# A fused layer-norm, spectral filter and bilinear block: 512-row gate products, GpSimd sums and one weight queue

## The chip, the cores and the metric

The kernel runs on one core of a Trainium2 chip. Time is device time in microseconds (us). A profile adds one traced execution with its own span, 1.7 to 2.2 us shorter than the device time of the same run. Most executions of one kernel agree within 0.3%. A run counts as slow when it lies more than 1.5% above the fastest of the same kernel; every comparison below uses fast runs alone, and every traced execution was a fast one.

In the profile PE is TensorE (matrix products), PEld its weight loads, DVE is VectorE, ACT is ScalarE, POOL is GpSimd, SP is the engine that issues most transfers. L964 is line 964 of that kernel's file, so one and the same statement has different numbers in different kernels.

## The reference

```python
def _A_ref(x, w_r, w_i):                 # x: 1 x 2048 x 640, filter: 2048 x 321
    X = rfft2(x.astype(f32)) * (w_r + 1j * w_i)
    return irfft2(X, s=(S, D)).astype(bf16)

def _B_ref(x, w_gate, w_up, w_down):     # 640 x 1536, 640 x 1536, 1536 x 640
    h = (x @ w_gate) * (x @ w_up)
    return h @ w_down

xn = layernorm(x)                        # over the 640 columns
out = x + _A_ref(xn, w_r, w_i) + _B_ref(xn, w_gate, w_up, w_down)
```

There are 2048 rows, worked on as 16 blocks of 128. "Gate products" below means the products with both `w_gate` and `w_up`; "bilinear product" means the elementwise `g * u` on VectorE.

## The kernel before

The kernel doesn't leave order to chance: it registers some hundreds of tasks (with engine, estimated duration, priority, what they read and write, and which PSUM banks they take), and its own planner, at build time, simulates the engines and fixes **one instruction order per engine**. On the chip each engine runs its list in that order and waits on semaphores. PSUM banks (8 of them, used singly or as 4 pairs) are handed out in the plan too, and a class of tasks may have a cap on how many it holds at once:

```python
sch = _Sched()
sch.caps = {"glu": opts.get("cap_glu", 2), "acc": opts.get("cap_acc", 4), "fill": 1}
...                                                # in plan(), for each task that could go next:
cap = self.caps.get(t.cls)
if cap is not None and held_by_cls.get(t.cls, 0) >= cap:
    continue
```

The phases on TensorE: warm-up products with zeros; transposes of the normalised blocks 0 to 3; the row transform (R); a spectral stage of 16 blocks, each a first transform (D), a second one (C, 321 columns), a multiplication by the filter on VectorE, sums, and an inverse product (IA); the second inverse stage (I) with a lot of VectorE work; and the down products, which also add the last spectral product. **Gate products are the filler**: they have the lowest priority and take what the other stages leave free, until they run out. Then the down products begin.

The gate products, as they were, for two blocks (256 rows), gate and up side by side in one bank:

```python
_CHUNKS = ((0, 1), (1, 1), (2, 2), (4, 2), (6, 2), (8, 2), (10, 2), (12, 2), (14, 2))   # (first block, blocks)
...
for w in range(2):                                 # gate, up
    for j in range(5):                             # 640 = 5 x 128
        ins = c.e.matmul(ps[:, bk, w * n:(w + 1) * n], v_gw[:, w, j, ft, :],
                         v_xt[:, j, rows], start=(j == 0), stop=(j == 4))
```

The sums of one spectral block, all on VectorE, behind that block's five multiplications:

```python
def em_cb(c, r2=r2):
    p00, p01, p10, p11 = (v_p[:, r2, 0, 0], ...)
    c.e.tensor_tensor(v_y[:, r2, 512:768], p01[:, 0:256], p10[:, 0:256], _OP.add)              # large
    c.e.scalar_tensor_tensor(v_y[:, r2, 896:961], p01[:, 256:321], -1.0, p10[:, 256:321], ...) # small
    c.e.tensor_tensor(v_y[:, r2, 768:833], p00[:, 256:321], p11[:, 256:321], _OP.subtract)     # small
    return c.e.tensor_tensor(v_y[:, r2, 256:512], p00[:, 0:256], p11[:, 0:256], _OP.subtract)  # large
```

The weight loads, gate weights on SP's queue, the first three of the up weights on ScalarE's:

```python
dma("ld_gw%d_%d" % (f0, w_), ..., q="act" if w_ and i < 3 else "sp")
```

Of the kernel before, what the change touches and what calls it, by code (L numbers as in the profile page):

```python
# [15 lines left out]
_DMA_LAT = 1300.0  # L16
_DMA_ISSUE = 520.0
# [53 lines left out]
class _Sched(object):  # L71
# [81 lines left out]
    def plan(self, nbanks=8, filler_deadline=0.0):  # L153
# [8 lines left out]
        eng_free = dict((e, 0.0) for e in _ENGS)  # L162
# [334 lines left out]
_OP = AluOpType  # L497
# [8 lines left out]
_CHUNKS = ((0, 1), (1, 1), (2, 2), (4, 2), (6, 2), (8, 2), (10, 2), (12, 2), (14, 2))  # L506
_LP = 321
_SN = math.sin(2.0 * math.pi / 5.0)
# [20 lines left out]
def _d_dve_tt16(n):  # L529
    return n * 0.52 + 75.0  # L530
# [16 lines left out]
def _build(nc, A_x, A_w_r, A_w_i, B_w_gate, B_w_up, B_w_down, out, opts=None):  # L547
# [3 lines left out]
    with es:  # L551
# [8 lines left out]
        sch.caps = {"glu": opts.get("cap_glu", 2), "acc": opts.get("cap_acc", 4), "fill": 1}  # L560
        lay = {}
# [43 lines left out]
        b_p = alloc("P", 2 * 4 * 2 * _LP)  # L605
        b_y = alloc("Y", 2 * 1024)
# [49 lines left out]
        v_p = V("P").bitcast(_F32).rearrange("p (r w c l) -> p r w c l", r=2, w=2, c=2)  # L656
        v_y = V("Y").rearrange("p (r n) -> p r n", r=2)
# [57 lines left out]
        dma("ld_sm1", v_sm[:, 1:3, :], d_sm[:, 1:3, :], 128 * 512, [(b_sm, ("t", 1, 3))], prio=0.25)  # L715
# [38 lines left out]
        for gi, (b0, nb) in enumerate(_LN_GROUPS):  # L754
            pbase = 1.0 + 0.05 * gi if gi < 4 else opts.get("ln_prio", 5.99) + 0.05 * (gi - opts.get("ln_lead", 3))
            for b in range(b0, b0 + nb):
                if b >= opts.get("act_stats", 8):
                    def em_sm(c, b=b):
                        return c.e.activation(v_jk, v_x[:, b, :], _ACTF.Copy, scale=1.0 / _D,
                                              accum_out=v_m32[:, b:b + 1])  # L760
                    T("sm%d" % b, "act", _d_act(640) + 93, em_sm, reads=[(b_x, ("s", b, b + 1))],
                      writes=[(b_m32, ("b", b, b + 1)), (b_jk, None)], prio=pbase)

                    def em_sq(c, b=b):
                        return c.e.activation(v_jk, v_x[:, b, :], _ACTF.Square, scale=-1.0, bias=v_m32[:, b:b + 1],
                                              accum_out=v_ss[:, b:b + 1])
                    T("sq%d" % b, "act", _d_act(640) + 186, em_sq,
                      reads=[(b_x, ("s", b, b + 1)), (b_m32, ("b", b, b + 1))],
                      writes=[(b_ss, ("b", b, b + 1)), (b_jk, None)], prio=pbase)
                else:  # L770
                    bns = []
                    for i in range(2):
                        def em_bn(c, b=b, i=i):
                            return c.e.bn_stats(v_st[:, b, 6 * i:6 * i + 6], v_x[:, b, 320 * i:320 * i + 320])  # L774
                        bns.append(T("bn%d_%d" % (b, i), "dve", 420.0, em_bn, reads=[(b_x, ("s", b, b + 1))],
                                     writes=[(b_st, ("b", 2 * b + i, 2 * b + i + 1))], prio=pbase))
                    if b == 1:
                        bns[0].deps.add(muls[0])
                        bns[1].deps.add(e0_first)

                    def em_ag(c, b=b):
                        return c.e.bn_aggr(v_mv[:, b, :], v_st[:, b, :])
                    T("ag%d" % b, "dve", 176.0, em_ag, reads=[(b_st, ("b", 2 * b, 2 * b + 2))],
                      writes=[(b_mv, ("b", b, b + 1))], prio=pbase)
            if b0 >= opts.get("act_stats", 8):
                def em_mb(c, sl_=slice(b0, b0 + nb)):
                    c.e.tensor_copy(v_mv[:, sl_, 0], v_m32[:, sl_])
                    return c.e.tensor_scalar(v_mv[:, sl_, 1], v_ss[:, sl_], 1.0 / _D, None, _OP.mult)
                T("mb%d" % b0, "dve", 211.0, em_mb, reads=[(b_m32, ("b", b0, b0 + nb)), (b_ss, ("b", b0, b0 + nb))],
                  writes=[(b_mv, ("b", b0, b0 + nb))], prio=pbase)  # L790
# [74 lines left out]
        for g in range(8):  # L865
            b = 2 * g
            gr = g % 2
            pf = opts.get("f_prio", 6.0) + 0.05 * g
# [67 lines left out]
        for i, (f0, nf) in enumerate(_GW_LOADS):  # L936
            for w_ in range(2):
                dma("ld_gw%d_%d" % (f0, w_), v_gw[:, w_, :, f0:f0 + nf, :].rearrange("p j r f -> p j (r f)"),
                    gvs[w_][:, :, f0 * 128:(f0 + nf) * 128], 5 * 128 * nf * 256,
                    [(b_gw, ("s", w_ * _NGW + f0, w_ * _NGW + f0 + nf))], prio=(0.004, 0.012, 0.022, 0.032, 0.05)[i] + 0.001 * w_,  # L940
                    q="act" if w_ and i < 3 else "sp")
        w_at = [6.0 + 2.2 * min(ft // 2, 4) for ft in range(12)]
        c_at = [6.3 + 2.2 * (b0 + nb - 1) for b0, nb in _CHUNKS]
        units = sorted((max(c_at[ci], w_at[ft + 1]), ci, ft) for ci in range(len(_CHUNKS)) for ft in range(0, 12, 2))
        for ui, (at_, ci, ft0) in enumerate(units):
# [5 lines left out]
            pe_ = 5.0 + 0.001 * ui  # L951
            for u in range(2):
                ft = ft0 + u

# [19 lines left out]
            def em_h(c, ft0=ft0, rr=rr, n=n, rows=rows):  # L974
                return c.e.tensor_tensor(v_ht[:, ft0:ft0 + 2, rows], v_gbf[:, rr, :, 0:n], v_gbf[:, rr, :, n:2 * n],  # L975
                                         _OP.mult)
            T("H_%d" % ui, "dve", _d_dve_tt16(2 * n), em_h,
              reads=[(b_gbf, ("r", 2 * rr, 2 * rr + 2))],
              writes=[(b_ht, ("col", b0, b0 + nb))], prio=pe_)
# [6 lines left out]
        for t in range(16):  # L986
            pq = 10.0 + 0.05 * t
            ar = t % 3
            r2 = t % 2
# [41 lines left out]
            def em_wm(c, tc=tc, r2=r2, wr=wr):  # L1031
                bk = bank_of(tc)
                ins = None
                for h in range(2):
# [3 lines left out]
                    for w in range(2):  # L1038
                        c.e.tensor_tensor(  # L1039
                            v_p[:, r2, w, :, 128 * h:128 * h + 128].rearrange("p c (m k) -> p c m k", k=4),  # L1040
                            xh.rearrange("p c (m k) -> p c m k", k=4), wv[:, w].unsqueeze(1).to_broadcast([128, 2, 32, 4]), _OP.mult)
                ins = c.e.tensor_tensor(  # L1042
                    v_p[:, r2, :, :, 256:321], ps[:, bk:bk + 2, 256:321].unsqueeze(1).to_broadcast([128, 2, 2, 65]),
# [4 lines left out]
                   writes=[(b_p, ("r", r2, r2 + 1))], prio=pq - 0.001, frees=tc)  # L1048
            hold(tc, wm)

            def em_cb(c, r2=r2):
                p00, p01, p10, p11 = (v_p[:, r2, 0, 0], v_p[:, r2, 0, 1], v_p[:, r2, 1, 0], v_p[:, r2, 1, 1])

                c.e.tensor_tensor(v_y[:, r2, 512:768], p01[:, 0:256], p10[:, 0:256], _OP.add)  # L1054
                c.e.scalar_tensor_tensor(v_y[:, r2, 896:961], p01[:, 256:321], -1.0, p10[:, 256:321], _OP.mult,
                                         _OP.subtract)
                c.e.tensor_tensor(v_y[:, r2, 768:833], p00[:, 256:321], p11[:, 256:321], _OP.subtract)
                return c.e.tensor_tensor(v_y[:, r2, 256:512], p00[:, 0:256], p11[:, 0:256], _OP.subtract)  # L1058
            T("CB_%d" % t, "dve", 2 * _d_dve(256) + 2 * _d_dve(65), em_cb,
              reads=[(b_p, ("r", r2, r2 + 1))], writes=[(b_y, ("r", 2 * r2, 2 * r2 + 1))], prio=pq - 0.001)  # L1060

            def em_ng(c, r2=r2):
                c.e.activation(v_y[:, r2, 0:256], v_y[:, r2, 512:768], _ACTF.Copy, scale=-1.0)  # L1063
                c.e.activation(v_y[:, r2, 833:896], v_y[:, r2, 897:960], _ACTF.Copy, scale=-1.0)
                return c.e.activation(v_y[:, r2, 961:1024], v_y[:, r2, 769:832], _ACTF.Copy)
            T("NG_%d" % t, "act", _d_act(256) + 2 * _d_act(63), em_ng,
              reads=[(b_y, ("r", 2 * r2, 2 * r2 + 1))], writes=[(b_y, ("r", 2 * r2 + 1, 2 * r2 + 2))],
              prio=pq - 0.001)

            def em_ia(c, t=t, r2=r2):  # L1070
                bk = bank_of(c.t)
                ins = None
                for k in range(5):
                    if k < 4:
                        l1, l2 = v_y[:, r2, 256 + k:768:4], v_y[:, r2, k:512:4]
                    else:
                        l1, l2 = v_y[:, r2, 768:896], v_y[:, r2, 896:1024]
# [4 lines left out]
            ia = T("IA_%d" % t, "pe", 10 * _d_mm(128), em_ia, reads=[(b_y, ("r", 2 * r2, 2 * r2 + 2)), (b_wd, ("e", 256 * t, 256 * t + 256))],  # L1082
# [14 lines left out]
        for a in range(16):  # L1097
            pa = 19.0 + 0.05 * a
# [71 lines left out]
        for a in range(16):  # L1170
            pc = 41.0 + 0.05 * a
# [3 lines left out]
            for hf in range(2):  # L1175
# [14 lines left out]
                def em_iv(c, ag2=ag2, a=a, sl3=sl3):  # L1190
# [3 lines left out]
                       reads=[(b_v, ("a", a, a + 1)), (b_sm, ("t", 1, 3))], prio=pc + 0.01 + 0.001 * hf - 22.0, after=[ag2])  # L1194

                def em_f1(c, ag2=ag2, a=a, xs=xs, sl3=sl3):
# [3 lines left out]
                       reads=[(b_xr, ("r", xs, xs + 1))], writes=[(b_out, ("r", ro, ro + 1))], prio=pc - 0.001,  # L1200
# [6 lines left out]
        sch.slack["dve"] = opts.get("slack_dve", 300.0)  # L1207
        sch.affinity = opts.get("affinity", 1500.0)
        sch.dma_bw = float(opts.get("dma_bw", 330.0))
        sch.plan(8, filler_deadline=opts.get("fill_deadline", 7000.0))  # L1210
# [77 lines left out]
```

## Time and profile before

| | kernel before |
|---|---|
| device time, median (range) | 210.78 us (210.69 to 210.83, 4 runs beside the changed kernel) |
| span of the traced execution | 209.1 us, clock 1.00 |
| TensorE, VectorE, ScalarE, GpSimd busy | 96%, 88%, 59%, 0% |
| first gate product | 7.38 us |
| spectral stage on TensorE: first D, last IA | 87.1, 140.8 us |
| last gate product | 145.2 us |

The prediction below shows the lines that carry most of this. One more is needed later, for the stretch from 90 to 125 us of the kernel before. It gives the stretch and its length, then busy us and instructions of TensorE, its weight loads, VectorE, ScalarE and GpSimd, then the granted clock, the DMA share and GB/s.

```profile
90.00:125.00 35.00, 34.42 (x383) 30.21 (x380) 33.89 (x112) 30.65 (x82) 0.00 (x0) 1.00 0.27 61
```

In the spectral stage TensorE (34.42 of 35) and VectorE (33.89) are both full. Such a line can't say which of the two is the bound; only what happens when one is relieved can.

### The profile page before, as it was taken

The page shows a single profiled execution, that of the slowest core. Times are in us where ns is not written, and L with a number is a line of the kernel's source. Part 1 is how long each engine was busy: PE and PEld are TensorE (multiplying, and loading weights), DVE is VectorE, ACT ScalarE, POOL GpSimd, SP SyncE. Part 2 cuts the span into 40 slices and gives each one's busy share as a digit, 9 for nine tenths or more (in the row PEclk, how much of TensorE's full clock was granted, in tenths as well). Part 3 has the DMA queues.
Part 4 walks back from the last instruction along what each step waited for, and adds up shares of the span by engine and source line. Part 5 has one row for each costly group of instructions (what it writes and reads, how often), then busy time and mean ns, then how long its engine had stood idle before and what let it go on. Part 6 is the DMA issues. An engine that isn't in the chain of part 4 may idle for free.

```text
span 209.1 us, 5208 instructions
## 1 busy us (share of the span) xinstructions
PE 201.7 (96%) x2044; PEld 170.5 (82%) x2044; DVE 184.3 (88%) x536; ACT 122.3 (59%) x281; POOL 0.2 (0%) x4
## 2 busy tenths in 40 slices
PE   7789999999999999989999999999999999999994
PEld 8689889988898998979888889898777776777773
DVE  4599999999999999389999999965999999999941
ACT  2276799899985666878998998888422022000000
POOL 0000000000000000000000000000000000000000
PEclk9999999999999999999999999999999999999999
DMA  6999983032011666102224223025022233223311
GB/s 178 301 340 391 383 113 68 5 63 58 9 31 35 141 198 178 33 17 57 52 57 122 53 61 103 0 66 157 3 75 71 78 110 110 56 88 110 91 55 47
DMA packets 30600, 21.74 MB, mean 104 GB/s; under 512 B 10480, under 2 KB 29552, under 8 KB 30448
## 3 DMA queue, kind: packets, MB, share of 16 engines
q1 hardware_dynamic: 28464, 20.40, 35.9%
q10 hardware_dynamic: 2112, 1.02, 1.9%
q8 instruction: 16, 0.26, 0.5%
q14 instruction: 8, 0.07, 0.1%
HBM read 16.82 MB, written 2.62 MB: 93 GB/s over the span
## 4 chain that ended last, share of the span: by engine, by line
PE 77%; DVE 9%; SPq 6%; DMA 5%; issue 2%; ACT 1%; DVEq 0%
PE ps L960 44%; PE ps L1183 17%; SPq L705 6%; DMA arena<-c_sm 5%; PE ps L921 2%; PE ps L1080 2%; PE ps L1079 2%; PE ps L1003 2%; PE ps L1191 1%; PE ps L1108 1%; PE ps L1024 1%; PE ps L1027 1%; PE ps L1026 1%; PE ps L1025 1%; DVE arena L1198 1%
## 5 line engine op out<-in xcount | busy, mean ns | idle before, releaser
L711 ACT ACTIVATE arena<-ps 128x512 bf16<-128x512 f32 (+5 forms) x190 | 100.6, 570 | 48.7 <-PE ps L960 21.8
L960 PE MATMUL ps<-arena 128*128 128x256 bf16 (+1 forms) x1080 | 112.0, 261 | 2.8 <-DMA arena<-in_B_w_gate_dram 1.0
L960 PEld LDWEIGHTS ps<-arena 128*128 128x128 bf16 x1080 | 93.7, 98 | 13.7 <-DMA arena<-in_B_w_gate_dram 1.9
L1183 PE MATMUL ps<-arena 128*128 128x320 bf16 x384 | 56.4, 299 | 0.0
L1183 PEld LDWEIGHTS ps<-arena 128*128 128x128 bf16 x384 | 37.3, 98 | 14.3 <-DVE arena L1198 0.2
L975 DVE TENSOR_TENSOR arena<-arena 128x512 bf16<-128x512 bf16 (+1 forms) x54 | 20.9, 389 | 9.5 <-ACT arena L711 9.3
L1039 DVE TENSOR_TENSOR arena<-ps,arena 128x256 f32<-128x256 f32 x64 | 22.6, 415 | 0.0
L1198 DVE TENSOR_TENSOR arena<-ps,arena 128x320 bf16<-128x320 f32 x32 | 15.4, 482 | 5.1 <-PE ps L1191 5.1
L1080 PE MATMUL ps<-arena 128*128 128x128 bf16 x80 | 10.7, 219 | 0.0
L1079 PE MATMUL ps<-arena 128*128 128x128 bf16 x80 | 10.6, 219 | 0.0
L774 DVE BATCH_NORM_STATS2 arena<-arena 128x6 f32<-128x320 bf16 x16 | 7.2, 478 | 3.4 <-DMA arena<-in_A_x_dram 3.2
L1079 PEld LDWEIGHTS ps<-arena 128*128 128x128 bf16 x80 | 8.8, 112 | 0.3
L1191 PE MATMUL ps<-arena 128*128 128x320 bf16 x32 | 8.9, 299 | 0.0
L874 DVE TENSOR_TENSOR arena<-arena 128x384 f32<-128x384 bf16 x16 | 8.8, 552 | 0.0
L1080 PEld LDWEIGHTS ps<-arena 128*128 128x128 bf16 x80 | 8.7, 112 | 0.1
L1042 DVE TENSOR_TENSOR arena<-ps,arena 128x260 f32<-128x260 f32 x16 | 7.0, 439 | 0.0
L1054 DVE TENSOR_TENSOR arena<-arena 128x256 bf16<-128x256 f32 x16 | 6.7, 420 | 0.2
L1063 ACT ACTIVATE arena<-arena 128x256 bf16<-128x256 bf16 x16 | 6.6, 411 | 0.4 <-DVE arena L1058 0.3
L875 DVE TENSOR_TENSOR arena<-arena 128x256 f32<-128x256 bf16 x16 | 6.7, 418 | 0.0
L1058 DVE TENSOR_TENSOR arena<-arena 128x256 bf16<-128x256 f32 x16 | 6.7, 417 | 0.0
L1163 DVE TENSOR_TENSOR arena<-arena 128x640 bf16<-128x640 f32 x8 | 6.5, 816 | 0.1
L1003 PE MATMUL ps<-arena 128*128 128x128 bf16 (+1 forms) x80 | 6.6, 219 | 0.0
(69 smaller groups left out, 208.1 us busy)
## 6 DMA issues: line engine op xcount, KB each, us to landing
arena<-in_A_x_dram SPq DMA_DIRECT2D x20, 160.0 KB, 2.4
out_dram<-arena SPq DMA_DIRECT2D x32, 80.0 KB, 1.6
arena<-c_tf SPq DMA_DIRECT2D x4, 384.0 KB, 10.9
arena<-in_A_w_r_dram SPq DMA_DIRECT2D x32, 40.1 KB, 2.3
arena<-in_A_w_i_dram SPq DMA_DIRECT2D x32, 40.1 KB, 2.2
arena<-in_B_w_gate_dram SPq DMA_DIRECT2D x4, 320.0 KB, 7.6
arena<-in_A_x_dram SPq DMA_DIRECT2D x1, 1280.0 KB, 12.2
arena<-c_ti SPq DMA_DIRECT2D x2, 512.0 KB, 4.7
```

The lines of the kernel that those rows point to most:

```text
L705: return c.e.dma_start(dst, src)
L711: return c.e.activation(dst, src, _ACTF.Copy)
L874: c.e.tensor_tensor(uo[:, o, :, 0:3, :], v_xb[:, b:b + 2, 0:6:2, :], v_xb[:, b:b + 2, 5:10:2, :], op)
L960: ins = c.e.matmul(ps[:, bk, w * n:(w + 1) * n], v_gw[:, w, j, ft, :], v_xt[:, j, rows], start=(j == 0), stop=(j == 4))
L975: return c.e.tensor_tensor(v_ht[:, ft0:ft0 + 2, rows], v_gbf[:, rr, :, 0:n], v_gbf[:, rr, :, n:2 * n], _OP.mult)
L1003: ins = c.e.matmul(psflat[:, bk * 512 + k * 128: bk * 512 + k * 128 + n], v_uq[:, k, t, :], v_fd[:, k * 128: k * 128 + n], start=True, sto ...
L1039: c.e.tensor_tensor(v_p[:, r2, w, :, 128 * h:128 * h + 128].rearrange("p c (m k) -> p c m k", k=4), xh.rearrange("p c (m k) -> p c m k", k ...
L1079: c.e.matmul(dst, l1, v_ti[:, t, 0, :], start=True, stop=False)
L1080: ins = c.e.matmul(dst, l2, v_ti[:, t, 1, :], start=False, stop=True)
L1183: ins = c.e.matmul(ps[:, bk, 0:320], v_ht[:, ft, a * 128:(a + 1) * 128], v_wd[:, ft, sl3], start=(ft == 7), stop=False)
L1191: return c.e.matmul(ps[:, bank_of(ag2), 0:320], v_sm[:, 2, :], v_v[:, a, sl3], start=False, stop=True)
L1198: return c.e.tensor_tensor(v_out[:, a % 2, sl3], ps[:, bk, 0:320], v_xr[:, xs, sl3], _OP.add)
```

## The change

The intent: fewer instructions on TensorE for the same gate work; VectorE relieved by an engine that stands idle; and gate weights in the order in which they are needed. In the plan this comes with third buffers and retuned constants. The core of the diff:

```diff
-_CHUNKS = ((0, 1), (1, 1), (2, 2), (4, 2), (6, 2), (8, 2), (10, 2), (12, 2), (14, 2))
+_CHUNKS = ((0,1),(1,1),(2,2),(4,4),(8,4),(12,4))
...
+                if nb == 4:                       # a bank holds gate or up for 512 rows
+                        for j in range(5):
+                            ins = c.e.matmul(ps[:, bk, :], v_gw[:, w, j, ft, :], v_xt[:, j, rows], ...)
...
+            def em_cd(c, ar=ar):                  # the two small sums, VectorE
+                c.e.scalar_tensor_tensor(v_y[ar][:, 896:961], ...)
+                return c.e.tensor_tensor(v_y[ar][:, 768:833], ...)
+            cd = T("CD_%d" % t, "dve", ...)
+            def em_cb(c, ar=ar):                  # the two large sums
+                c.e.tensor_tensor(v_y[ar][:, 512:768], p01[:, 0:256], p10[:, 0:256], _OP.add)
+                return c.e.tensor_tensor(v_y[ar][:, 256:512], p00[:, 0:256], p11[:, 0:256], _OP.subtract)
+            ce = opts.get("cb_eng", "pool")
+            T("CB_%d" % t, ce, ..., after=[cd])
...
-                    q="act" if w_ and i < 3 else "sp")
+                    q="act" if w_ and i < 1 else "sp")
...
+        sch.caps["a"] = opts.get("cap_a", 2)      # transforms may hold 2 of the 4 PSUM pairs
-        b_p = alloc("P", 2 * 4 * 2 * _LP)         # products of a block: a third buffer
+        b_p = alloc("P", 3 * 4 * 2 * _LP)
+        b_y3 = alloc("Y3", _YS, at=lay["STAT"][0])   # spectrum of a block: a third buffer
-        dma("ld_sm1", ..., prio=0.25)             # table of the first transform product: earlier
+        dma("ld_sm1", ..., prio=0.055)
...                                                # and of the planner's constants:
-_DMA_LAT = 1300.0
+_DMA_LAT = 1000.0
+_START = 680.0
-        sch.slack["dve"] = opts.get("slack_dve", 300.0)
-        sch.affinity = opts.get("affinity", 1500.0)
+        sch.slack["dve"] = opts.get("slack_dve", 600.0)
+        sch.slack["pe"] = opts.get("slack_pe", 1500.0)
+        sch.affinity = opts.get("affinity", 300.0)
...
```

Cut: some more constants of this kind (priorities of the normalisation and of the row transform, the end of the fillers, the assumed DMA rate and issue time), and the statistics of blocks 6 and 7, which go from VectorE to ScalarE.

> **What bounds the kernel now.** I read the page first, then the products by shape, then the chain of work that ended last, then TensorE's timeline at the start and in the middle, then busy time by stretches.
>
> ```profile
> span 209.1 us, 5208 instructions
> PE 201.7 (96%) x2044; PEld 170.5 (82%) x2044; DVE 184.3 (88%) x536; ACT 122.3 (59%) x281; POOL 0.2 (0%) x4
> ```
>
> TensorE (PE) is busy 96% of the span, VectorE (DVE) 88%, GpSimd (POOL) nothing. The run takes 210.76 us, 1.66 more than the span. "Busy" can hide slack, since pipelined products overlap, so I take the pace of products from unbroken runs in the chain of waits:
>
> ```profile
> 37.33 0.56 PE ps L921 x10
> 70.85 6.55 PE ps L960 x60
> 176.35 1.63 PE ps L1183 x12
> ```
>
> Columns: start, length, what. Ten 128-column products take 0.56 us (56 ns each), sixty 256-column gate products 6.55 (109.2 ns), twelve 320-column down products 1.63 (135.8 ns). All three fit columns / 2.4 + 2.5 ns. So TensorE's own need is a sum. Gate: 840 x 109.2 + 240 x 56 ns = 105.1 us. Down and last spectral product: 416 x 135.8 = 56.5. Other 128-column products (transposes, four transform stages): 420 x 56 = 23.5. The 64 of 321 columns, 136.5 ns apart in the timeline: 8.7. Together 193.8 us, at a granted clock of 1.00.
>
> The rest of the span is loss, and TensorE's timeline at the start shows half of it (the bracket is idle time and what ended it):
>
> ```profile
> 6.59 0.22 PE L729 MATMUL ps<-arena 128*128 128x128 bf16 x1
> 7.38 1.29 PE L960 MATMUL ps<-arena 128*128 128x128 bf16 x20 [0.57 <-DVE arena L795]
> 9.66 1.29 PE L960 MATMUL ps<-arena 128*128 128x128 bf16 x20 [0.98 <-DMA arena<-in_B_w_gate_dram]
> 10.78 0.44 PE L835 MATMUL ps<-arena 128*128 128x128 bf16 x5
> 11.84 2.48 PE L960 MATMUL ps<-arena 128*128 128x128 bf16 x40 [0.61 <-DVE arena L782]
> ...
> 24.24 0.73 PE L921 MATMUL ps<-arena 128*128 128x128 bf16 x10 [0.25 <-DMA arena<-c_sm]
> ```
>
> Before 7.38 us there are only warm-up products, fillers (L729) and one transpose. Comparing start-to-start with the pace above, the issue stream then loses 1.16 us before 9.66, 0.78 before 11.84, about 0.4 in small pieces, and 0.41 before 24.24: 2.75 us. After 25 us I find only 0.74 at 91, 0.40 at 147, 0.49 at 173 and three small ones: about 2 us. From the last product's issue end (206.2) to the end, 2.9 us go to the last sum and store. Check: 7.38 + 193.5 (one transpose came earlier) + about 5 + 2.9 = 208.8, against 209.1. **TensorE's instruction stream is the bound, with about 5 us of gaps, a 7.4 us start and a 2.9 us tail.**
>
> VectorE is close behind. Busy us by stretch (TensorE, its loads, VectorE, ScalarE, GpSimd):
>
> ```profile
> 100.00:120.00 20.00, 20.00 (x224) 17.59 (x223) 19.26 (x64) 18.52 (x51) 0.00 (x0) 1.00 0.31 71
> 160.00:180.00 20.00, 19.67 (x163) 14.28 (x161) 19.96 (x49) 3.90 (x6) 0.00 (x0) 1.00 0.33 95
> ```
>
> In both VectorE is full (19.26 and 19.96 of 20), but TensorE hardly waits for it: gate products fill its time in the first, down products in the second.
>
> **What the Trainium skill says.** "TensorE: Matmul & The Clock Gate", section "Back-to-back issue gap": warm gap N/2.4 + 2.5 ns. The trace agrees at 128, 256 and 320 columns. The same section also gives a sustained 131 ns for 512 columns; a rate that beats one column a cycle is not in this trace (256 columns take 109.2 ns), so I don't use it. "GPSIMD Engine Reference", section "3.1 Elementwise — side-by-side cycle accounting": about 2.6 cycles per element at 1.2 GHz for two inputs. No arithmetic of GpSimd is in this trace. "SBUF — State Buffer", section "Who interferes with whom": a VectorE instruction with two SBUF inputs and a GpSimd one that reads SBUF exclude each other for a whole instruction. Not visible yet. "DMA: Bandwidth & Descriptors", section "Queues, rings and completion order": each DMA engine takes turns between queues that have work. The trace agrees: the first gate weights were issued at 1.66 us and landed 5.7 us later, with three loads of the ScalarE queue competing.
>
> **The change part by part.**
>
> *512-row gate products.* Blocks 4 to 15 go from 720 products of 256 columns to 360 of 512; columns stay. Estimate for one from the fitted pace: 213.3 + 2.5 = 215.8 ns instead of 218.4 for two. 360 x 2.6 ns = **0.9 us** off the path, surely. Evictions stay at 512 columns each, and the bilinear products on VectorE stay 42 of 512 and 12 of 256 columns. A cost: the gate needs four transposed blocks before it can start on them. Gate work on blocks 0 to 3 lasts about 26 us, until roughly 36; statistics of blocks 6 and 7 move to ScalarE and normalisation gets earlier, so I expect blocks 4 to 7 ready by 30.
>
> *Sums on GpSimd.* Two 256-element sums per spectral block leave VectorE:
>
> ```profile
> L1054 DVE TENSOR_TENSOR arena<-arena 128x256 bf16<-128x256 f32 x16 | 6.7, 420 | 0.2
> L1058 DVE TENSOR_TENSOR arena<-arena 128x256 bf16<-128x256 f32 x16 | 6.7, 417 | 0.0
> ```
>
> That is 13.4 busy us (0.34 us each start-to-start, 10.8 us of VectorE's time). Estimate for GpSimd: 256 x 2.6 / 1.2 = 0.55 us (from the page) plus dispatch, say 0.7; two make 1.4 us a block, 22 us in all, on an idle engine. A block's chain grows by about 0.7 us, covered by third buffers for products and spectrum. VectorE's 3.3 us a block becomes about 2.6, so this stage is squeezed and the inverse stage begins earlier. But TensorE is already full there; the total of its work is unchanged. **Gain on the path: part of the 2 us of later gaps, I take 0.4.**
>
> *Queue and load order.* Only the first up-weights stay on ScalarE's queue. Ahead of the first gate tile come then about 1.0 MB (two blocks of x, two weight loads, the identity) instead of about 1.6. The first 5.2 us moved 178 GB/s x 5.2 = 0.93 MB, so it lands near 5.6 us rather than 7.4. Then the first transpose and its eviction (to 6.46 us) are what holds the gate: start at about 6.7, **0.7 us** gained. Weights for feature tiles 2 and 3 follow by about 7.5, so the 1.16 us gap goes; the second block's normalisation (done at 9.25 in this trace) then leaves about 0.7 us idle. Of 1.16 + 0.78 + 0.4 some 1.5 should go. The table for the first transform product is loaded before the large x load: most of 0.41 goes, I take 0.3. Sum **2.5 us**, half of it sure.
>
> Total: 0.9 + 0.4 + 2.5 = 3.8, so 207.0. Planner constants retuned with it favour slightly more; I say **206.9**.
>
> **Rivals.** (1) *GpSimd becomes a wait.* Port exclusion makes VectorE's bilinear products wait up to 0.7 us each and the spectral chain slips. For: about 30 such products lie in that stage. Against: the multiplications read one operand from PSUM, and even 30 x 0.3 = 9 us would only eat what was freed. If it bound, the inverse stage would start later and VectorE, full from 142 to about 200 us, would hold the last products: 208 to 211. (2) *Starved early.* The four-block chunk or x behind weights on a single queue leaves a new gap of 1 to 3 us at 10 to 40 us: 208 to 210. (3) *VectorE was the bound.* Then 10.8 us freed would bring 5 us or more. Against: TensorE hardly waited for it; the floor 6.7 + 192.9 + 2.9 + 1.66 = 204.2 us forbids it. (4) *Start is hidden anyway*: x still arrives too late; only 0.9 to 1.5 us gained: about 209.5.
>
> **Range and chances.** The floor, 204.2, needs no gaps at all, so I put the low end at 204.9. The high end, 208.9, is the sure 0.9 plus about a microsecond, or a full gain eaten partly by a new gap. 2% faster means below 206.5, which needs gaps of about 2.3 us after the start, near my estimate: 0.42. Slower by 2% would need 4 us of new waits on a stream that is now dense: 0.02.
>
> **What would show it.** 512-column gate products 216 ns apart; first gate product near 6.7 us; no wait for gate weights at 9.66 or for the transform table at 24; GpSimd busy some 22 us, its sums 0.6 to 0.8 us; VectorE busy near 172 us; first inverse product before 142; TensorE's issue loss after its start about 2.5 us instead of 5. The prediction fails if GpSimd's sums take 1.5 us or more, if a gap above 1 us opens between 25 and 145 us, or if the first gate product stays at 7.4.

## The result, and the profile after

| | before | after |
|---|---|---|
| device time, median (range, runs) | 210.78 (210.69 to 210.83, 4) | 208.14 (207.81 to 208.20, 4) |
| span of the traced execution | 209.1 | 206.0 |
| first gate product | 7.38 | 6.65 |
| first D, last IA | 87.1, 140.8 | 90.2, 137.8 |
| last gate product, first I | 145.2, 142.0 | 143.1, 138.9 |

The ratio is 0.9872, with a 95% interval of 0.9855 to 0.9889. Ratios here are the mean time of one kernel's fast runs over that of the other's of the same rounds, so not quite the ratio of the medians. **The change gains 1.3%: within 2%, and within the predicted range.**

The head of the page of the changed kernel:

```profile
span 206.0 us, 4467 instructions
PE 199.0 (97%) x1667; PEld 135.5 (66%) x1682; DVE 178.2 (87%) x507; ACT 121.4 (59%) x282; POOL 21.8 (11%) x36
```

Loads of weights on TensorE fall from 2044 to 1682: 360 of the 362 are the 512-row products' (720 became 360). The records of products (1667) are fewer than the loads: 15 of the 360 are missing from this trace, which matters below. VectorE loses 6 us and GpSimd gains 21.6.

In the chain of waits an unbroken run of the new products reads (start, length, what):

```profile
67.14 6.47 PE ps L964 x30
```

Thirty products in 6.47 us are 215.7 ns each, where the prediction had 215.8.

TensorE's timeline at the start (start, length of the group, line; the bracket is idle time and what ended it):

```profile
6.65 1.28 PE L984 MATMUL ps<-arena 128*128 128x128 bf16 x20
8.68 1.28 PE L984 MATMUL ps<-arena 128*128 128x128 bf16 x20 [0.75 <-DMA arena<-in_B_w_up_dram]
9.93 0.45 PE L839 MATMUL ps<-arena 128*128 128x128 bf16 x5
10.95 1.93 PE L984 MATMUL ps<-arena 128*128 128x128 bf16 x30 [0.57 <-DVE arena L799]
...
19.41 5.85 PE L984 MATMUL ps<-arena 128*128 128x256 bf16 x52 [0.65 <-DVE arena L1001]
```

The start is earlier by 0.73 us. A wait for weights is still there: it now names the up weights instead of the gate weights. The wait at 10.95 is for the second block's transposed copy. The wait before 19.41 is new. It ends with a bilinear product (L1001), and that product was late because its engine stood at a load. VectorE's and ScalarE's timelines show two such waits:

```profile
9.09 0.49 DVE L778 BATCH_NORM_STATS2 arena<-arena 128x6 f32<-128x320 bf16 x1 [1.01 <-DMA arena<-in_A_x_dram]
9.50 0.37 DVE L821 TENSOR_SCALAR arena<-arena 128x640 bf16<-128x640 bf16 x1
```

```profile
16.84 0.74 ACT L763 ACTIVATE arena<-arena 128x640 bf16<-128x640 bf16 x1 [1.02 <-DMA arena<-in_A_x_dram]
```

At 9.09 VectorE had stood 1.01 us for block 2's rows; behind that, in the fixed order, stood block 1's scaling (9.50), ready about a microsecond before. At 16.84 ScalarE stands 1.02 us for the load of blocks 4 to 7, which had been issued at 9.02, 7.8 us earlier. VectorE stands there too, for 0.70.

Three stretches of the changed kernel, with the columns as before:

```profile
90.00:125.00 35.00, 34.59 (x311) 23.25 (x316) 31.58 (x105) 31.09 (x85) 16.41 (x25) 1.00 0.27 60
100.00:120.00 20.00, 19.79 (x189) 13.65 (x190) 18.13 (x60) 18.70 (x51) 10.47 (x16) 1.00 0.33 75
160.00:180.00 20.00, 20.00 (x161) 14.72 (x160) 20.00 (x50) 2.60 (x4) 0.00 (x0) 1.00 0.31 88
```

TensorE stays full in all three. VectorE has a little air in the spectral stage (31.58 of 35, before 33.89).

The sums in the changed kernel, from the table of groups by form (count, then busy us and mean ns, then idle time before them):

```profile
L1088 POOL TENSOR_TENSOR arena<-arena 128x256 bf16<-128x256 f32 x16 | 10.3, 645 | 112.9 <-DVE arena L1081 112.9
L1089 POOL TENSOR_TENSOR arena<-arena 128x256 bf16<-128x256 f32 x16 | 11.9, 744 | 0.0
L1079 DVE SCALAR_TENSOR_TENSOR arena<-arena 128x65 bf16<-128x65 f32 x16 | 3.6, 227 | 0.3
L1081 DVE TENSOR_TENSOR arena<-arena 128x65 bf16<-128x65 f32 x16 | 3.6, 224 | 0.0
```

The sums take 0.64 and 0.74 us on GpSimd, 0.42 each before on VectorE.

**Where the 3 us went**, from the two traces. The pace of a product is columns / 2.4 + 2.5 ns; loss is the time between starts beyond that. The 15 missing records leave apparent holes of 216 ns each, 3.2 us, and are taken out. The useful work contains 0.3 us of transposes that run before the first gate product.

| us | before | after | difference | predicted |
|---|---|---|---|---|
| useful work of TensorE | 193.8 | 192.9 | -0.9 | -0.9 |
| first gate product | 7.38 | 6.65 | -0.7 | -0.7 |
| loss from there to 25 us | 2.7 | 3.0 | +0.3 | -1.8 |
| loss after 25 us | 2.6 | 0.9 | -1.7 | -0.4 |
| tail | 2.9 | 2.9 | 0 | 0 |
| sum | | | -3.0 | -3.8 |

The spans differ by 3.1 us, the medians by 2.6. The traced execution of the changed kernel is the fastest of its four (207.81 us; the others 208.13 to 208.20), so the traces flatter it by some 0.3 us.

### The profile page after: what moved, and what is told of

Read it like the earlier page. It is cut to its first block, busy times and chain, and to the rows that moved or that the text cites. A ratio compares the mean times of both kernels' runs of the same rounds, so it can differ in the third digit from the quotient of the medians.

```text
span 206.0 us, 4467 instructions
## 1 busy us (share of the span) xinstructions
PE 199.0 (97%) x1667; PEld 135.5 (66%) x1682; DVE 178.2 (87%) x507; ACT 121.4 (59%) x282; POOL 21.8 (11%) x36
## 4 chain that ended last, share of the span: by engine, by line
PE 86%; DMA 4%; SPq 4%; DVE 4%; issue 1%; ACT 0%; DVEq 0%
PE ps L964 36%; PE ps L1216 25%; PE ps L984 9%; DMA arena<-in_A_x_dram 4%; SPq L709 4%; PE ps L1141 2%; PE ps L925 2%; PE ps L1224 2%; PE ps L1112 2%; PE ps L1029 2%; PE ps L1113 2%; DVE arena L1065 1%; PE ps L1050 1%; PE ps L1053 1%; PE ps L1052 1%; PE ps L1051 1%
## 5 line engine op out<-in xcount | busy, mean ns | idle before, releaser
L715 ACT ACTIVATE arena<-ps 128x512 bf16<-128x512 f32 (+6 forms) x182 | 96.7, 567 | 48.5 <-PE ps L1141 22.6
L964 PE MATMUL ps<-arena 128*128 128x512 bf16 x345 | 80.3, 379 | 0.8
L964 PEld LDWEIGHTS ps<-arena 128*128 128x128 bf16 x360 | 33.8, 98 | 36.5 <-ACT arena L715 1.4
L1216 PEld LDWEIGHTS ps<-arena 128*128 128x128 bf16 x384 | 37.3, 98 | 14.1
L984 PE MATMUL ps<-arena 128*128 128x128 bf16 (+1 forms) x360 | 27.9, 237 | 2.0 <-DMA arena<-in_B_w_up_dram 0.8
L984 PEld LDWEIGHTS ps<-arena 128*128 128x128 bf16 x360 | 25.2, 98 | 4.0 <-ACT arena L715 1.5
L1000 DVE TENSOR_TENSOR arena<-arena 128x512 bf16<-128x512 bf16 x36 | 15.4, 427 | 8.8 <-ACT arena L715 8.7
L1088 POOL TENSOR_TENSOR arena<-arena 128x256 bf16<-128x256 f32 x16 | 10.3, 645 | 112.9 <-DVE arena L1081 112.9
L1089 POOL TENSOR_TENSOR arena<-arena 128x256 bf16<-128x256 f32 x16 | 11.9, 744 | 0.0
L1112 PEld LDWEIGHTS ps<-arena 128*128 128x128 bf16 x80 | 8.7, 112 | 1.7
L1113 PEld LDWEIGHTS ps<-arena 128*128 128x128 bf16 x80 | 8.7, 112 | 1.4
L778 DVE BATCH_NORM_STATS2 arena<-arena 128x6 f32<-128x320 bf16 x12 | 5.6, 484 | 4.4 <-DMA arena<-in_A_x_dram 4.2
L769 ACT ACTIVATE arena<-arena 128x640 bf16<-128x640 bf16 x10 | 8.3, 826 | 0.0
L763 ACT ACTIVATE arena<-arena 128x640 bf16<-128x640 bf16 x10 | 7.3, 729 | 1.0 <-DMA arena<-in_A_x_dram 1.0
L1001 DVE TENSOR_TENSOR arena<-arena 128x256 bf16<-128x256 bf16 (+1 forms) x18 | 6.0, 332 | 1.5 <-ACT arena L715 1.5
```

The costliest lines, as they stand in the source:

```text
L715: return c.e.activation(dst, src, _ACTF.Copy)
L964: ins = c.e.matmul(ps[:, bk, :], v_gw[:, w, j, ft, :], v_xt[:, j, rows], start=(j == 0), stop=(j == 4))
L1000: return c.e.tensor_tensor(v_ht[:, ft0, rows], v_gbf[:, rr, 0, :], v_gbf[:, rr, 1, :], _OP.mult)
L1088: c.e.tensor_tensor(v_y[ar][:, 512:768], p01[:, 0:256], p10[:, 0:256], _OP.add)
L1089: return c.e.tensor_tensor(v_y[ar][:, 256:512], p00[:, 0:256], p11[:, 0:256], _OP.subtract)
L1112: c.e.matmul(dst, l1, v_ti[:, t, 0, :], start=True, stop=False)
```

## The experiments

There are two kinds. In a **same-order** run the changed kernel's plan stays as it is, and one thing is moved or replaced in the finished lists. In a run **planned anew**, one setting changes and the planner makes a new order for everything, so it measures the setting and the new plan together. The kernel before ran beside each (210.78 to 210.90 us).

**1. The 512-row products alone (same order).** Each 512-column product becomes two of 256.

```diff
-for j in range(5):
-    matmul(ps[:, bk, :], v_gw[:, w, j, ft, :], v_xt[:, j, rows], ...)
+for h in range(2):
+    r0 = rows.start + 256 * h
+    for j in range(5):
+        matmul(ps[:, bk, 256*h:256*h+256], v_gw[:, w, j, ft, :], v_xt[:, j, r0:r0+256], ...)
```

> The changed kernel with the same planned order on every engine; only each 512-row gate product of blocks 4 to 15 is issued as two of 256 rows into the same bank (360 products more). Theory (TensorE's stream is the bound, each product costs 2.5 ns over its columns): 0.9 us slower than the changed kernel, about 209.05 us, 0.990 to 0.993 of before; 256-row products 109.2 ns apart. Rival (the product length is hidden behind evictions or the gain lies in the plan): no change, 208.1 us.

Measured: median 210.05 us (208.37 to 211.91; five fast runs of six), ratio 0.9952 (0.9921 to 0.9983), span 206.8. The chain of waits of this run has

```profile
67.68 6.55 PE ps L966 x60
```

which is 109.2 ns a product, 218.3 for what took 215.7. Over 360 products that is 0.9 us, as expected. The spans differ by 0.8 us too, but by chance: in this trace the first gate product comes 0.7 us later (7.36), and the losses are 0.8 us smaller. The timed runs say more (0.8% of 210.8, 1.7 us), but they scatter as no other kernel's here (fast runs from 208.37 to 210.56), and only one was traced. The 0.9 us is shown by the pace in the traces; why the runs scatter stays open.

**2. The large sums back on VectorE (same order).** Each pair of large sums goes into VectorE's list right behind that block's small sums; GpSimd's list is emptied.

```diff
 sch.plan(8, ...)
+for t in list(sch.order["pool"]):
+    cd = [d for d in od if d.name == "CD_" + t.name[3:]][0]      # od: VectorE's list
+    od.insert(od.index(cd) + 1, t); t.eng = "dve"
```

> The changed kernel with the planned order of all engines kept, only the two 256-element sums of each block are moved from GpSimd to VectorE, directly behind the small sums of that block. Theory: VectorE, busy 31 of 40 us between 100 and 140 us, gets 10.8 us more in that stage and overflows, the spectral chain slips and TensorE, whose order is fixed, waits: 210 to 211 us. Rival (TensorE alone is the bound, the move is worth nothing): 208.1 to 208.5 us.

Measured: 214.72 us, ratio 1.0187 (1.0174 to 1.0200). That is 6.6 us above the changed kernel, far more than either side expected. The stretch of 100 to 120 us and, in the list of waits of the whole execution (us, count, longest), TensorE's at VectorE's filter multiplications (L1068):

```profile
100.00:120.00 20.00, 16.25 (x151) 10.96 (x154) 19.66 (x65) 15.39 (x43) 0.00 (x0) 1.00 0.27 59
```

```profile
PE ps L964 <- DVE arena L1068: 3.6, 4, 1.7
```

VectorE is full (19.66 of 20) and TensorE is not (16.25): in *this* order VectorE is the bound of the stage.

**3. The same, planned anew.**

```diff
-ce = opts.get("cb_eng", "pool")
+ce = opts.get("cb_eng", "dve")
```

> The changed kernel with the two large sums on VectorE and everything planned anew for that. Theory: the planner fills TensorE with gate products again, and only the later gaps of the kernel before (about 1.6 us) come back: 209.0 to 209.8 us. Rival A (the move is the whole gain): 210.5 us or more. Rival B (worth nothing): 208.1 us.

Measured: 217.39 us, ratio 1.0317 (1.0298 to 1.0335). The theory failed; the time is beyond the whole gain that rival A named. The last gate product comes at 138.8, before the last inverse product of the spectral stage (147.6): the filler ran out. The stretch of 140 to 160 us, and TensorE's timeline in it, where inverse products wait for ScalarE's copy (L1098), the step behind the sums:

```profile
140.00:160.00 20.00, 14.32 (x118) 11.01 (x117) 14.55 (x39) 9.05 (x20) 0.00 (x0) 0.74 0.21 58
```

```profile
143.90 0.25 PE L1112 MATMUL ps<-arena 128*128 128x128 bf16 x1 [2.06 <-ACT arena L1098]
146.77 0.29 PE L1112 MATMUL ps<-arena 128*128 128x128 bf16 x1 [1.89 <-ACT arena L1098]
```

Nothing fills these waits, and the granted clock in the stretch falls to 0.74. Here the spectral stage ends 9 us after the gate products; in the changed kernel it ends 5 us before them (137.8 and 143.1).

**4. The queue alone (same order).** Two loads of up weights go back to ScalarE's queue.

```diff
+for name in ("ld_gw4_1", "ld_gw2_1"):              # right behind ld_gw0_1
+    os_.remove(t); oa.insert(oa.index(f) + 1, t)   # SP's list to ScalarE's
```

> The changed kernel with the same planned order of compute; only the second and third loads of the up weights go back from SyncE's to ScalarE's queue. Theory: the first gate product goes back from 6.65 to about 7.4 us because these loads again share bandwidth with the first tile's weights, while the wait before the next gate tile at 8.7 us shrinks: 0.2 to 0.7 us slower, about 208.6. Rival (the start is hidden by the second block's normalisation): 208.1 us.

Measured: 208.72 us, ratio 0.9898 (0.9885 to 0.9910). TensorE's timeline:

```profile
7.45 1.29 PE L984 MATMUL ps<-arena 128*128 128x128 bf16 x20 [0.62 <-DVE arena L799]
9.69 1.29 PE L984 MATMUL ps<-arena 128*128 128x128 bf16 x20 [0.95 <-DMA arena<-in_B_w_gate_dram]
```

The old start (7.45) and the old wait for gate weights are back. The queue is worth about 0.55 us by the ratios (0.9898 less 0.9872 of 210.8; their intervals just overlap), 0.8 us by the starts of these two traces. The direct effect shows in every trace: the first gate weights land at 6.10 to 6.49 us in the nine with the new queue, at 6.85 to 7.90 in the five with the old one.

**5. All old planner settings (planned anew).** The rest of the change stays; constants, priorities and the table's load are as before, and the line with the cap is gone.

```diff
-sch.caps["a"] = opts.get("cap_a", 2)
-_DMA_LAT = 1000.0; _START = 680.0; slack dve 600, pe 1500; affinity 300; ...
+_DMA_LAT = 1300.0; _START = 0.0;   slack dve 300, pe 1000; affinity 1500; ...
```

> The changed kernel with every planner constant and priority of the kernel before (load latency, start and issue time, normalisation and transform priorities, statistics of blocks 6 and 7 on VectorE, slacks, affinity, bandwidth, filler deadline, no cap on paired banks, late load of the transform table); 512 rows, GpSimd sums and the single queue stay. Theory: TensorE's sum of work stays 0.9 us under that of before and the first gate product early, but gaps of the old plan may return: 208.2 to 209.8 us. Rival (the retuned constants are what gained): 210.5 us or more.

Measured: 223.61 us, ratio 1.0590 (1.0551 to 1.0629), **15.5 us** above the changed kernel. The rival's range held, not the theory's. The prediction had put all of these down as "slightly more".

**6 and 7. One part each on the kernel before (planned anew, old settings).** First the sums on GpSimd, then the 512-row products, each with the third buffers that the change gives them and without the cap.

```diff
 kernel before
+CB on GpSimd behind CD; third buffers for products and spectrum          # b_pool
+_CHUNKS = ((0,1),(1,1),(2,2),(4,4),(8,4),(12,4)); sums split, on VectorE  # b_rows512
```

> The kernel before plus only the sums on GpSimd (with the third buffers and the order behind the small sums): 256 rows, old queues, old constants, planned anew. Theory: in the kernel before TensorE hardly waits for VectorE, so freeing it is worth at most the later gaps: 209.3 to 210.6 us. Rival (VectorE was the bound, as the 6 to 9 us lost by taking the sums back from GpSimd would say): 204 to 207 us.

> The kernel before plus only the 512-row gate products of blocks 4 to 15 (sums on VectorE, old queues, old constants, planned anew; the buffers and the split of the sums in two tasks as in the changed kernel). Theory: 0.9 us less on TensorE, 209.9 us, if the plan still fits. Rival (four-block chunks delay the start of the spectral stage, gate products run out before VectorE's spectral chain ends, and TensorE then waits, as in the run with sums planned on VectorE): 212 us or more.

Measured: 222.49 us (ratio 1.0559, 1.0541 to 1.0578) and 225.83 us (1.0726, 1.0706 to 1.0746). Each alone makes the kernel 12 or 15 us *slower*. For b_pool both theories missed. For b_rows512 the time was the rival's, but not by its mechanism: gate products had not run out there (the last at 162 us, the spectral stage at 139). In the 30 us from 90 to 120 TensorE is busy for 21.96 in the first and for 17.23 in the second, while gate products are left to do. Something kept them from being placed there, and the cap was the suspect. In the second VectorE is full in the same stretch (29.28 of 30, in the first 24.81), so there it may be the bound instead; the 512-row products with the cap and the sums on VectorE were not run with the old settings, and run 7's 15 us stay unexplained.

**8. The cap alone (planned anew).**

```diff
-        sch.caps["a"] = opts.get("cap_a", 2)
```

> The changed kernel without one line, the planner's cap of two pairs of PSUM banks for the spectral stages, planned anew. Theory (the 222 to 224 us of the two runs with GpSimd sums and the old constants come from this: once VectorE no longer holds the spectral stages back, they hold three or four pairs of banks and gate products find none, so TensorE stands between 90 and 125 us and the gate products end near 155 us): 214 to 223 us. Rival (the load times, priorities or slacks of the old plan did it): 208 to 209.5 us.

Measured: 221.09 us (219.94 to 221.62), ratio 1.0477 (1.0454 to 1.0499). **One line of the planner is worth 13 us.** The stretch of 90 to 125 us in this run, for all engines and then for the gate products' line alone (busy us of products, of loads, then clock, DMA share, GB/s):

```profile
90.00:125.00 35.00, 25.40 (x246) 17.87 (x248) 26.97 (x88) 25.33 (x77) 14.74 (x22) 0.96 0.26 60
```

```profile
90.00:125.00 35.00, 6.04 (x24) 2.60 (x26) 0.96 0.26 60
```

and the gate products' line of the changed kernel in the same stretch:

```profile
90.00:125.00 35.00, 17.43 (x71) 6.77 (x75) 1.00 0.27 60
```

With the cap 75 weight loads of gate products lie in this stretch, without it 26, and TensorE is idle for 9.6 of 35 us. What it waits for there is mostly the spectral filter's loads:

```profile
PE ps L1049 <- DMA arena<-in_A_w_i_dram: 7.0, 7, 2.3
```

I read it so: the order puts spectral products one behind another, ahead of gate products that could run, and TensorE stands where each block's data is late. The expectation said that gate products find no free bank. That is how I read the planner, in which the cap does nothing but withhold banks from the transforms; the trace itself shows only the missing gate products and the waits.

**9. The cap given to run 6 (planned anew).**

```diff
 kernel before + GpSimd sums + third buffers
+sch.caps["a"] = opts.get("cap_a", 2)
```

> The kernel before with the sums on GpSimd, third buffers and that cap of two pairs (256 rows, old queues, all other old constants). Theory: the cap takes the gaps between 90 and 125 us away again, and freeing VectorE is then worth no more than the later gaps: 209 to 210.8 us. Rival A (VectorE was the bound and only the missing cap hid it): 204 to 207 us. Rival B (cap not the cause): about 222 us.

Measured: 210.75 us (210.49 to 211.60), ratio 0.9999 (0.9984 to 1.0015). The page:

```profile
PE 202.8 (97%) x2044; PEld 171.1 (82%) x2044; DVE 176.4 (84%) x506; ACT 120.9 (58%) x279; POOL 22.0 (10%) x36
```

VectorE's busy time fell from 184.3 to 176.4 us and the time did not move. Its loss after 25 us is 2.4 us, as before (2.6); the wait for the transform table, which in this trace ends at 25.15 us and costs 0.9, is left out of that. The loss sits elsewhere, though: the 0.75 us at 91 us are gone, and six gaps from 153 to 184 us make 1.8. **In the kernel before, relieving VectorE was worth nothing: TensorE was the bound.** That the third buffers are what makes the cap necessary (two buffers already keep the transforms from running ahead) fits runs 6 and 9, but no run has the third buffers alone, and run 7 wasn't repeated with the cap.

**10. The order behind the small sums (same order).** GpSimd's sums no longer wait for VectorE's two small sums of that block, only for its multiplications.

```diff
+for t in sch.order["pool"]:
+    t.deps = set(d for d in t.deps if d.name != "CD_" + t.name[3:])
```

> The changed kernel with the same planned order, but GpSimd's sums no longer wait for VectorE's small sums of that block, only for its multiplications. Theory (both engines read two SBUF inputs [...] and shut each other out for a whole instruction): the small sums, 0.22 us each, begin together with a GpSimd sum of 0.64 us and stretch to 0.5 to 0.9 us; GpSimd ends a block some 0.3 us earlier, but VectorE's chain pays about 0.5 us a block: 208.1 to 209.5 us. Rival (no exclusion): small sums stay at 0.22 us, total 207.8 to 208.1 us.

Measured: 213.43 us, ratio 1.0120 (1.0107 to 1.0133), 5.3 us slower than the changed kernel. The mechanism was expected, its size was not. The small sums, by form and then in the timeline around 103 us, with GpSimd's sum beside them:

```profile
L1079 DVE SCALAR_TENSOR_TENSOR arena<-arena 128x65 bf16<-128x65 f32 x16 | 5.9, 366 | 0.3
L1081 DVE TENSOR_TENSOR arena<-arena 128x65 bf16<-128x65 f32 x16 | 10.7, 671 | 0.0
```

```profile
103.12 0.69 DVE L1079 SCALAR_TENSOR_TENSOR arena<-arena 128x65 bf16<-128x65 f32 x1
103.73 0.77 DVE L1081 TENSOR_TENSOR arena<-arena 128x65 bf16<-128x65 f32 x1
```

```profile
102.95 0.77 POOL L1088 TENSOR_TENSOR arena<-arena 128x256 bf16<-128x256 f32 x1 [1.18 <-DVE arena L1068]
```

A sum of 65 elements that takes 0.22 us alone takes 0.67 beside GpSimd: in the lines above it ends when GpSimd's instruction does (103.81 and 103.72). Sixteen blocks of it raise VectorE's busy time from 178.2 to 189.2 us. VectorE is close to full in this stage (33.24 of 35 from 90 to 125), so the delay comes through: TensorE has 30.26 busy us between 90 and 125 instead of 34.59.

**11. The second block's scaling first (same order).** If the wait at 10.95 us comes from VectorE standing at block 2's load, block 1's scaling put ahead of it should remove it.

```diff
+od.remove(m1); od.insert(od.index(b2), m1)     # mul1 ahead of bn2_0 in VectorE's list
```

> The changed kernel with the same planned order, but on VectorE the scaling of block 1 stands ahead of the statistics of block 2, which wait for its load. Theory (the 0.73 us loss before the second block's gate products is VectorE standing at a load while block 1 could be scaled, 1.4 us earlier): the loss shrinks to 0.1 to 0.4 us, total 207.5 to 207.9 us. Rival (the next weights or the later wait at 18.5 us take it back): 208.1 us.

Measured: 208.05 us (207.45 to 208.22), ratio 0.9862 (0.9848 to 0.9877). TensorE's timeline:

```profile
7.08 2.65 PE L984 MATMUL ps<-arena 128*128 128x128 bf16 x40
9.56 0.44 PE L839 MATMUL ps<-arena 128*128 128x128 bf16 x5
10.55 1.93 PE L984 MATMUL ps<-arena 128*128 128x128 bf16 x30 [0.54 <-DVE arena L799]
...
19.33 5.85 PE L984 MATMUL ps<-arena 128*128 128x256 bf16 x52 [0.80 <-DVE arena L1001]
```

VectorE's copy of the second block's transposes (L839):

```profile
10.04 0.36 DVE L716 COPY arena<-ps 128x384 bf16<-128x384 bf16 x1
```

The theory failed: the loss before the second block's gate products is 0.71 us, and was 0.73. On TensorE the transposes stand right in front of the gate products that need their copy (9.56, copy to 10.40, 10.55). That order causes the wait: run 12, which moves the transposes forward on TensorE, has none at this place. VectorE's standing cost at most the 0.14 us that TensorE lost before the transposes at 9.93. The product behind the wait does come 0.40 us earlier (10.55, 10.95), though the first gate product comes 0.43 us later (7.08, 6.65). Most of that is the wait for the up weights, which landed at 8.36 instead of 8.59 without any load having been moved. At the next long wait it is gone: the same 52 products follow at 19.33 and at 19.41, released by the bilinear product that waits for blocks 4 to 7. The time gains nothing that the scatter would let one see.

**12. Seven such moves (same order).** No engine is to stand at a late load with ready work behind it.

```diff
+move("pe", "T0_1", "GU_2_0");    move("act", "eT0_1_act", "eG_1_0")
+move("dve", "mul1", "bn2_0");    move("dve", "eT0_1_dve", "bn2_0")
+move("act", "sm6", "sq6");       move("dve", "H_5", "bn5_0");   move("dve", "H_6", "ag4")
```

> The changed kernel with seven places of the planned order moved so that no engine stands at a late load of x while other work is ready: block 1's transpose before the second gate tile on TensorE, its scaling and eviction before block 2's statistics, statistics of block 6 on ScalarE behind the evictions, two bilinear products before the statistics of blocks 4 and 5. Theory: 0.7 us of loss before the second block and about 0.8 at 18.5 us go: 206.5 to 207.2 us. Rival (the loads only move the wait elsewhere): 208.0 us.

Measured: 208.10 us (207.70 to 208.47), ratio 0.9872 (0.9854 to 0.9889): equal to the changed kernel. The timeline:

```profile
7.61 1.28 PE L984 MATMUL ps<-arena 128*128 128x128 bf16 x20
9.52 0.45 PE L839 MATMUL ps<-arena 128*128 128x128 bf16 x5 [0.63 <-DVE arena L821]
```

The rival was right about the outcome: the waits only move. Block 1's transposes now wait for its scaling (0.79 us lost before 9.52), and 0.6 us are lost before 21.81 instead of 0.8 before 19.41. The loss from the first gate product to 25 us fell to 2.4 us (3.0 in the changed kernel), but the first gate product came at 7.61 in this trace instead of 6.65. I put that start down to the warm-up, which varies from run to run (see the last section): in the nine traces with the new queue the first gate product comes at 6.65 us where TensorE's pace doubles at 3.80, at 7.08 where it doubles at 5.72, and at 7.61 here, where it doubles at 6.99. A later start also swallows later waits. So I add the two, first gate product and loss to 25 us: 9.66 in the changed kernel, 9.57 in run 11 and 9.98 in run 12, against 9.92, 9.92 and 9.37 in runs 1, 2 and 10, which move nothing there. The moves of runs 11 and 12 show no gain. So no version was found that clearly beats the changed kernel.

## Why the prediction was right, and where its steps were not

**The bound.** Right for the kernel before: run 9 relieves VectorE by 8 us for nothing. In the changed kernel TensorE's work, start and tail still make about 202 of 206.0 us. Rival 3 (VectorE was the bound) falls for the kernel before.

**512-row products, 0.9 us.** Right: 215.7 ns for 218.3, in the trace. The four-block chunk didn't starve TensorE: before the first such product on record, at 37.9 us, there is only the 216 ns hole of a missing one.

**The start, 0.7 us.** Right in these two traces (7.38 to 6.65), about 0.55 us in the times of run 4, and in part luck. 6.65 is the earliest start of nine traces with the new queue (up to 7.61). And the step "so it lands near 5.6 us" was wrong: the first gate weights landed at 6.37. That cost nothing only because the transposed copy was not done before 6.37 either. The wait for the table at 24 us is gone, as predicted.

**The early gaps, mis-sized.** The step "Weights for feature tiles 2 and 3 follow by about 7.5, so the 1.16 us gap goes" failed. Those up weights were issued at 2.70 and landed at about 8.6 us, 5.9 us later. Until then 1.96 MB had moved (228 GB/s over 8.59 us), while these weights and all data loads issued before them make 1.67 MB: some 0.3 MB, most of it of loads issued behind them, had come first. So a place further forward in one queue bought less than bytes divided by the rate, which is how the prediction had reckoned, for the first gate weights too. 0.9 us of loss stayed there. The 0.7 us for the second block came as predicted. And 0.8 us is new at 18.5, where two engines stand at the load of blocks 4 to 7; rival 2 had named such a gap. With the table this term was to bring -1.8; it brought +0.3. Start and early gaps together were to gain 2.5 us and gained 0.4: rival 4 (x arrives too late anyway) was nearer here. In run 11 too the load of blocks 4 to 7 decides when the products at 19.3 us start.

**The later gaps, mis-sized the other way.** "Part of the 2 us of later gaps, I take 0.4" was put down to the sums on GpSimd. By the same working the trace of the kernel before has 2.6 us there, not 2. The loss fell by 1.7. Run 9 has the sums on GpSimd with the old constants and keeps 2.4 us of it; run 1, with the changed order, keeps 0.5. So the new plan as a whole closed these gaps, not the sums alone; which setting did it is not separated. The two errors, 2.1 and 1.3 us, have opposite signs, and the sum missed by 0.8 us in the spans and 1.2 in the medians.

**GpSimd's part.** Durations (0.6 to 0.8 us) and total (21.8 us) were right. VectorE's busy time was to fall to 172 us and is 178.2. Rival 1 (port exclusion) hardly happens in the changed kernel: one collision stands out, a bilinear product of 0.63 us at 115.4 where others take 0.42. Run 10 shows one reason: the order behind the small sums keeps these clear of it, and without that order the kernel is 5.3 us slower. I had spoken of the multiplications and the bilinear products and not of this ordering, though it is in the change's description.

**What the prediction missed altogether** is that the parts don't add. It summed 0.9, 0.4 and 2.5 us. But on the kernel before, the sums on GpSimd are worth 0.0 (run 9), and in the changed kernel taking them back costs 6.6 us in the same order and 9.2 planned anew (runs 2 and 3). The changed plan starts the spectral stage 3 us later and ends it 3 us earlier, and with the sums on VectorE runs 2 and 3 did not keep that pace. And "planner constants retuned … favour slightly more" hid a line that is worth 13 us (run 8). The total came out near because all parts were present at once, and because the errors in the early and the later gaps partly cancelled: that part is luck.

## What to carry to other kernels

Where instruction order is fixed at build time, read a diff's limits on buffers and banks as carefully as its instructions: GpSimd's sums with third buffers cost 12 us without a cap, and nothing with it. An engine that is not the bound can be one step from it, so a part that is worth nothing alone may be what another part stands on; to price parts, undo each in the same order and try each alone. When work goes to another engine, look whether the two hold each other up, as in run 10; if so, put the short instructions of the old engine ahead of the moved ones, not beside them.

## What the Trainium skill lacked or had wrong

- "TensorE: Matmul & The Clock Gate", section "Back-to-back issue gap", gives a sustained 131 ns for products of 512 columns. In the changed kernel 316 pairs of such products, each with its own weight load, have starts 216 ns apart (median), which is the page's isolated formula. "What you observe" in its Part 1 has the pace of products double around 4 us into sustained work, give or take 0.5 us. Here, with the first warm-up product at about 1.05 us, the doubling (107 to 56 ns a product) came 2.8 us later in the changed kernel, after 26 products, and 5.9 us later in run 12; in runs 1, 2, 7, 8, 9 and 12 none of the 48 warm-up products was fast. The first gate product with the new queue moves with it, between 6.65 and 7.61 us, so a single trace's start is uncertain by about 1 us. The profile's granted clock reads 1.00 over all this, but that shows nothing: the traces hold no clock record before the doubling (in the kernel before the first one begins at 4.72 us, and the pace doubles at 4.75; the changed kernel's trace holds none at all).
- "GPSIMD Engine Reference", section "3.1 Elementwise — side-by-side cycle accounting", gives a cost per element and a total at 2048 elements, but nothing for a short instruction; for the call that starts one the page has only a rough "tens of cycles". At 256 elements the per-element figure makes an estimated 0.55 us; the trace shows means of 0.645 and 0.744 us, and 0.6 us from the start of the first sum to that of the second.
- No page that I read treats a cap on the PSUM banks that a latency-bound stage may hold in a fixed instruction order: without it 221.09 us, with it 208.14.
